# Turning the last third of x by DMA in units 5 and 6 of a fused hash-attention and SwiGLU kernel

## The chip, the cores and the metric

The kernel runs on one core of a Trainium2 chip. The metric is the device time of one execution in microseconds (us), lower is better. The engines are PE (TensorE, matrix multiplication; PEld is its weight load), DVE (VectorE), ACT (ScalarE), POOL (GpSimd) and SP (SyncE, which here only issues DMAs). Each engine works through its own queue in order; semaphores order work between engines.

## The reference, cut to what matters

```python
# q, k, v: 4 batches x 8 heads x 768 positions x 64; proj: 64 x 6
q_bucket, k_bucket = 6 sign bits of q @ proj and of k @ proj
scores = where(q_bucket == k_bucket, q @ k.T / 8, -1e9)
attn_out = softmax(scores) @ v                       # with 1e-9 in the denominator
x = attn_out as 3072 tokens x 512
xn = x / sqrt(mean(x * x) + 1e-6) * rms_g
out = (silu(xn @ w_gate) * (xn @ w_val)) @ w_out     # d_ff = 1536
```

The output is float32, 3072 x 512.

## The kernel before, in words

**Units.** The 3072 tokens are worked in eight units of 384 (half a batch each; `u` = 0 to 7). Attention for a unit runs over 8 heads, two heads making a pair (`hp` = 0 to 3). Each head takes three steps, so a unit has `NS` = 24 steps. In a step PE makes scores (L349), ACT exponentiates them (L361), and PE multiplies probabilities by v (L374) into `o_ps`. What a unit's attention leaves is `x[u]`, 128 partitions x 3 thirds x 512, so that a third (`c` = 0, 1, 2) is 128 tokens.

**From attention to x.** `attn_out` (L382) runs once for each pair: DVE adds a mean of v (L388) and takes a reciprocal (L393), then the engine handed in, POOL by default, multiplies (L395) into `x`. For pairs 0 to 2 POOL also makes the squares (L401), which DVE sums later (L417). For pair 3 DVE makes squares and sums itself (`sumsq_dve`, L411, one instruction for each third). If the engine is DVE, `attn_out` calls `sumsq_dve` at once; otherwise a later step, `s_step`, does. For the last pair of a unit `o_step` stands at step 2 of the next unit's 24 and `s_step` at step 4. Before the change only unit 0 and unit 7 hand DVE to the last pair.

**From x to xnT.** `norm` (step 4) sums the squares over pairs (L439), POOL takes the power -1/2 (L443), and DVE scales each third to float16 `xn`. The feed-forward part needs x transposed, `xnT`, with the gain vector `rms_g` multiplied in. There are two ways. `turn_x` lets PE transpose four 128x128 blocks into a PSUM bank (L467), which DVE evicts with the gain (L473). `turn_dma` lets SP issue one DMA transpose from `xn` to `xnT` (L431); then the gain is multiplied in by `norm` (L452 in place of L460). `ONDMA` says how many thirds of a unit go by DMA. They are issued at step 5, one behind the other on SP's queue.

**Feed-forward beside attention.** While unit u+1 runs its attention, PE works off a list of pieces: the output projection of unit u-1 (`project`, L513, nine pieces of four matmuls), the turns of unit u by PE, and then 24 gate and 24 value halves of unit u (L484). All 384 tokens of `xnT` are read by each gate matmul, so the first gate of a unit needs all three thirds. A planner, `spread`, gives each piece a cost (a projection piece 4 x 216, a turn 220, a gate half 324) and deals the pieces over the steps so that their sum grows evenly. For a third that goes by DMA in units below 6 an empty piece of cost 220 stands where the turn would be.

**Queues and buffers.** SP issues loads, the small sends of hash bits (L308), DMA transposes and stores (L526) in the order in which the program lists them. Projections, turns, gates, values, hashes and means take their PSUM banks in turn from a pool of three (`g`). `xnT` has two buffers, `xn` one.

Of the kernel before, what the change touches and what calls it, by code (L numbers as in the profile page):

```python
# [16 lines left out]
H = 8  # L17
# [16 lines left out]
def kernel(  # L34
# [388 lines left out]

    rstds = {}

    ONDMA = {2: 2, 3: 2, 4: 2, 5: 2, 6: 2, 7: 1}

    def turn_dma(u, c):
        if c == 0:
# [16 lines left out]
    def norm(u):  # L446
# [3 lines left out]
        for c in range(3 if 0 < u < 7 else 2):  # L450
            if c < ONDMA.get(u, 0):
                nc.vector.scalar_tensor_tensor(  # L452
# [141 lines left out]
    order = [(0, 0), (0, 1), (1, 0), (1, 1)]  # L594
# [3 lines left out]
    def at(w, s, f, *a):  # L598
        plan[NS * w + s].append(lambda: f(*a))
# [117 lines left out]
    TX = 37  # L717

    LAGS = (0, 0, 0, 0, 0, 1, 1)
    sqs = {}  # L720

    def o_step(u, hp, *eng):
# [12 lines left out]
    for n, (u, h) in enumerate(order):  # L735
        t = 3 * n + 4 - ((u, h) == (0, H - 1))
        for part in range(2):
            at(0, t + part, av, u, h, part)
        if h % 2:
            if (u, h) == (0, H - 1):  # L740

                at(0, t + 1, o_step, u, h // 2, nc.vector)
                at(0, t + 1, norm_scale, u)
                at(0, t + 1, nc.vector.tensor_scalar_mul, gcol, gcol, float(DMODEL) ** 0.5)
                at(0, t + 2, hash_only, 1, 1)
                at(0, t + 2, hash_signs, 1, 1)
                at(0, t + 2, norm, u)
                at(0, TX-1, norm_third, u, 2, nc.scalar.mul)
                at(0, TX + 1, send_pair, 1, 1)
                for c in range(3):  # L750
                    at(0, TX, turn_x, u, c, c == 2)
                continue
            if (u, h) == order[-1]:
                at(0, t + 1, o_step, u, h // 2, nc.vector)
                continue

            steps = [(t + 1, o_step), (t + (3 if h == 7 else 4 if u == 7 else 6), s_step)]
            for s, step in steps:
                if s < 2 * NS or s % NS in (2, 4) or (step is o_step and (u, h // 2) in AHEAD):
                    at(0, s, step, u, h // 2)  # L760
                else:
                    late.append((s, step, u, h // 2))
# [42 lines left out]
    def spread(t0, n, pieces):  # L805
        fixed = [SCORES + (AV if (t - 1) % 3 < 2 else 0) for t in range(t0, t0 + n)]
        extra = [(t, *inserts.pop(t)) for t in range(t0, t0 + n) if t in inserts]
        total = sum(fixed) + sum(p[0] for p in pieces) + sum(e[1] for e in extra)
        i, done = 0, 0
        for s in range(n):  # L810
            done += fixed[s]
            while i < len(pieces):
                weight, whole, steps = pieces[i]
                full = done + weight // 2 > total * (s + 1) // n
                if extra and whole and t0 + s >= extra[0][0] and (full or extra[0][1] > MEAN):
                    _, weight, *step = extra.pop(0)
                    place(t0 + s, step)
                    done += weight
                    continue
                if full:  # L820
                    break
                done += weight
                for delay, *step in steps:
                    at(0, t0 + s + delay, *step)
                i += 1
        for _, _, *step in extra:
            place(t0 + n - 1, step)
        assert i == len(pieces)

    for u in range(7):  # L830
# [9 lines left out]
        at(0, t0 + 4, norm, u)  # L840
        for c in range(ONDMA.get(u, 0)):
            at(0, t0 + 5, turn_dma, u, c)
        pieces = []
        for i in range(9):
# [5 lines left out]
            if i in (6, 7):  # L850
                thirds = ((0,), (1, 2))[i - 6]
                for c in thirds:
                    if c >= ONDMA.get(u, 0):
                        pieces.append((TURN, False, [(0, turn_x, u, c)]))
                    elif u < 6:
                        pieces.append((TURN, False, []))
        lag, after = LAGS[u - 1 : u + 1]
        spread(t0 + lag, NS + after - lag, pieces + gates)
# [89 lines left out]
```

## Time and profile before

| What | Value |
|---|---|
| median of 3 runs | 326.93 us (326.87 to 327.19) |
| the profiled execution's own time | 326.68 us |
| its span, first to last instruction | 324.9 us |
| mean granted TensorE clock | 0.999 |
| scores on PE (L349) | 384 matmuls |
| transposes of x on PE (L467) | 52 matmuls, 4.7 us busy, mean 219 ns |
| their evictions by DVE (L473) | 11, mean 688 ns |
| DMA transposes (L431) | 11, 1202 to 2021 ns each on SP |
| x by POOL (L395) | 30, mean 837 ns |
| x by DVE (L395) | 2, mean 558 ns |
| xn by DVE with the gain (L452) | 11, mean 748 ns |
| xn by DVE without it (L460) | 11, mean 615 ns |

The span runs from the first to the last instruction; the execution's own time also holds 1.78 us around it. Busy times of an engine are sums over its instructions. Matmuls overlap, so the mean of one is longer than its share of PE's time. In a timeline, rows that follow one another on one engine and line are merged (x4 is four instructions), and an idle time ahead of a row stands in brackets with what ended it.

### The profile page before, as it was taken

What the parts mean: (1) busy time and instruction counts of PE and PEld (TensorE: products, weight loads), DVE (VectorE), ACT (ScalarE), POOL (GpSimd) and SP (SyncE); (2) the same over time, 40 slices, a digit from 0 to 9 for tenths busy, and PEclk for the clock granted to TensorE, in tenths of its full rate; (3) what the DMA queues carried; (4) which work ended last, traced back from release to release, by engine and by line L of the source; (5) the groups of instructions that cost most, each with busy time, mean ns of one, the idle gap of its engine ahead of it and who ended that gap; (6) DMA issues with size and microseconds to landing.
All of it is one profiled execution on the core that took longest, in us unless ns stands there. A gap on an engine that the chain in (4) does not pass through costs nothing.

```text
span 324.9 us, 7772 instructions
## 1 busy us (share of the span) xinstructions
PE 319.9 (98%) x2955; PEld 194.4 (60%) x2955; DVE 229.7 (71%) x512; ACT 228.4 (70%) x333; POOL 157.6 (49%) x204
## 2 busy tenths in 40 slices
PE   8999999999999999999999999999999999999996
PEld 3676666656566565655566565655666556665554
DVE  5887876859888568874888568785677536673870
ACT  7999887667688676776767776777777768744322
POOL 4999759955974363731883621752582111221000
PEclk9999999999999999999999999999999999999999
DMA  7942999988428864055547056002100030003002
GB/s 208 360 168 85 226 216 195 192 159 151 103 38 158 157 136 88 6 94 156 89 100 145 35 125 120 7 5 66 72 4 3 1 99 34 0 2 105 10 2 97
DMA packets 85741, 32.63 MB, mean 100 GB/s; under 512 B 70908, under 2 KB 82632, under 8 KB 85704
## 3 DMA queue, kind: packets, MB, share of 16 engines
q1 hardware_dynamic: 81800, 27.35, 36.1%
q0 software_dynamic: 3680, 4.72, 8.5%
q8 instruction: 23, 0.38, 0.5%
q14 instruction: 14, 0.11, 0.1%
q10 hardware_dynamic: 224, 0.07, 0.1%
HBM read 28.58 MB, written 6.29 MB: 107 GB/s over the span
## 4 chain that ended last, share of the span: by engine, by line
PE 98%; ACT 1%; DVE 0%; issue 0%
PE s_ps L349 20%; PE g_ps L484 19%; PE v_ps L484 19%; PE y_ps L513 18%; PE o_ps L374 11%; PE d_ps L218 2%; PE t_ps L156 2%; PE d_ps L238 2%; PE z_ps L580 1%; PE x_ps L467 1%; PE y_ps L532 1%; PE m_ps L333 1%; ACT psb L361 1%; DVE kT L158 0%; PE s_ps L156 0%
## 5 line engine op out<-in xcount | busy, mean ns | idle before, releaser
L361 ACT ACTIVATE psb<-s_ps,ebias 128x768 f16<-128x768 f32 x192 | 167.7, 900 | 20.0 <-PE s_ps L349 19.2
L349 PE MATMUL s_ps<-QK 128*128 128x384 f16 (+1 forms) x384 | 93.5, 326 | 1.2 <-ACT psb L361 1.1
L492 ACT ACTIVATE t<-g_ps 128x384 f32<-128x384 f32 x96 | 47.2, 492 | 52.2 <-PE g_ps L484 50.5
L484 PE MATMUL g_ps<-xnT,wg 128*128 128x384 f16 x384 | 82.7, 326 | 0.0
L484 PE MATMUL v_ps<-xnT,wv 128*128 128x384 f16 x384 | 81.8, 326 | 0.0
L501 DVE SCALAR_TENSOR_TENSOR a<-t,g_ps 128x384 f32<-128x384 f32 x96 | 53.0, 552 | 28.9 <-ACT t L492 27.2
L395 POOL TENSOR_TENSOR x<-otmp,rcp 128x384 f32<-128x384 f32 x30 | 25.1, 837 | 96.2 <-DVE rcp L393 95.8
L513 PE MATMUL y_ps<-wo,ht 128*128 128x512 f16 x276 | 67.7, 379 | 0.0
L502 DVE SCALAR_TENSOR_TENSOR ht<-a,v_ps 128x384 f16<-128x384 f32 x96 | 53.2, 554 | 11.5 <-PE v_ps L484 3.6
L374 PEld LDWEIGHTS <-psb 128*128 128x128 f16 x1152 | 51.9, 97 | 15.7 <-issue 1.2
L374 PE MATMUL o_ps<-vl,psb 128*128 128x65 f16 x1152 | 55.8, 193 | 0.0
L349 PEld LDWEIGHTS <-QK 128*128 128x128 f16 (+1 forms) x384 | 34.8, 98 | 33.7 <-issue 7.9
L484 PEld LDWEIGHTS <-wg 128*128 128x128 f16 x384 | 35.2, 97 | 21.2
L484 PEld LDWEIGHTS <-wv 128*128 128x128 f16 x384 | 35.1, 97 | 20.8 <-issue 0.2
L513 PEld LDWEIGHTS <-ht 128*128 128x128 f16 x276 | 24.9, 98 | 23.0
L525 ACT COPY ysb<-y_ps 128x512 f32<-128x512 f32 x23 | 13.5, 587 | 15.8 <-PE y_ps L513 15.8
L388 DVE TENSOR_TENSOR otmp<-o_ps,cvb 128x390 f32<-128x390 f32 x32 | 17.8, 557 | 7.1 <-PE o_ps L374 7.1
L208 POOL CAST QK<-qT 64x768 f16<-64x768 f32 x20 | 16.5, 823 | 10.3 <-DVE qT L195 9.5
L401 POOL TENSOR_TENSOR sq<-x 128x384 f32<-128x384 f32 x24 | 19.9, 828 | 1.9
L208 POOL CAST QK<-kT 64x768 f16<-64x768 f32 x20 | 16.4, 822 | 5.2 <-DVE kT L195 3.1
L473 DVE TENSOR_TENSOR xnT<-x_ps,gcol 128x512 f16<-128x512 f16 x11 | 7.4, 688 | 15.1 <-PE x_ps L467 15.0
L195 DVE STREAM_TRANSPOSE kT<-kL 128x192 f32<-128x192 f32 x32 | 16.4, 516 | 0.0
(85 smaller groups left out, 274.9 us busy)
## 6 DMA issues: line engine op xcount, KB each, us to landing
vn<-in_v_dram SPq DMA_DIRECT2D x16, 384.0 KB
out_dram<-ysb SPq DMA_DIRECT2D x23, 256.0 KB
qL<-in_q_dram SPq DMA_DIRECT2D x40, 96.0 KB
kL<-in_k_dram SPq DMA_DIRECT2D x40, 96.0 KB
kn<-in_k_dram SPq DMA_DIRECT2D x5, 384.0 KB
qn<-in_q_dram SPq DMA_DIRECT2D x5, 384.0 KB
wg<-in_moe_w_gate_dram POOLq DMA_DIRECT2D x2, 768.0 KB, 9.4
wv<-in_moe_w_val_dram POOLq DMA_DIRECT2D x2, 768.0 KB, 11.7
```

Source lines behind the costliest of these rows:

```text
L208: nc.gpsimd.tensor_copy(QK[b, 2 * hp + hh, "h"][0:64, o : o + S], src[64 * hh : 64 * hh + 64, :])
L349: nc.tensor.matmul(ps[:, j, 0:HALF], QK[b, h, "h"][rows, S + jt * 128 : S + (jt + 1) * 128], QK[b, h, "h"][rows, half * HALF : (half + 1) ...
L361: nc.scalar.activation(psb[u, h][:, 2 * ch : 2 * ch + 2, :], sps.pop((u, i))[:, :, 0:HALF], AF.Exp, bias=ebias, scale=ESCALE,)
L374: nc.tensor.matmul(o[:, c, hh, 0:65], psb[u, h][:, jt, c * 128 : (c + 1) * 128], vls[b % 2][:, h, 2 * (jt % 3) + jt // 3 if b in PARITY el ...
L388: nc.vector.tensor_add(tmp[:, :, :, 0:65], o[:, :, :, 0:65], cvb[b % 2][:, 2 * hp : 2 * hp + 2, 0:65].unsqueeze(1).to_broadcast([128, 3, 2 ...
L395: eng.tensor_mul(xd.rearrange("p c (h d) -> p c h d", h=2), tmp[:, :, :, 0:64], r.to_broadcast([128, 3, 2, 64]),)
L401: eng.tensor_mul(sq, xd, xd)
L484: nc.tensor.matmul(ps, w[:, kt, fs], xnT[u][:, kt, :], start=(kt == 0), stop=(kt == 3))
L492: nc.scalar.activation(t, fbank[u, ft, "g_ps"], AF.Tanh, scale=0.5)
L501: nc.vector.scalar_tensor_tensor(out=a, in0=t, scalar=1.0, in1=g, op0=ALU.add, op1=ALU.mult)
L502: nc.vector.scalar_tensor_tensor(out=ht[u][:, ft, :], in0=a, scalar=0.5, in1=vv, op0=ALU.mult, op1=ALU.mult)
L513: nc.tensor.matmul(y, ht[u][:, ft, c * 128 : (c + 1) * 128], wo[:, ft, :], start=(ft == 0), stop=(ft == NF - 1),)
```

## The change

Two edits. First, units 5 and 6 turn all three thirds of x by DMA. Their third `c` = 2 leaves `turn_x` and goes to `turn_dma`, as a third DMA transpose behind the other two at step 5; `norm` therefore scales it with the gain. In unit 5 an empty piece keeps the turn's place in the plan; in unit 6 (`u < 6` is false) none does. Second, for the last pair of units 5 and 6 `o_step` is handed DVE: DVE multiplies x and then makes the squares and their sums at once at step 2, and there is no `s_step` at step 4.

```diff
-    ONDMA = {2: 2, 3: 2, 4: 2, 5: 2, 6: 2, 7: 1}
+    ONDMA = {2: 2, 3: 2, 4: 2, 5: 3, 6: 3, 7: 1}
...
     LAGS = (0, 0, 0, 0, 0, 1, 1)
+
+    XDVE = (5, 6)
     sqs = {}
...
-            if (u, h) == order[-1]:
+            if (u, h) == order[-1] or u in XDVE and h == H - 1:
                 at(0, t + 1, o_step, u, h // 2, nc.vector)
                 continue
```

## The prediction

> **What bounds the kernel now.** I read the totals and the chain that ended last first, because they say whether any engine but PE can matter.
>
> ```profile
> PE 319.9 (98%) x2955; PEld 194.4 (60%) x2955; DVE 229.7 (71%) x512; ACT 228.4 (70%) x333; POOL 157.6 (49%) x204
> ...
> PE 98%; ACT 1%; DVE 0%; issue 0%
> ```
>
> PE is busy 319.9 of 324.9 us, and 98% of the chain is PE's own work, one instruction behind the other. So PE time that is taken out shortens the span one for one, and a new wait on PE lengthens it one for one. Work added to DVE, POOL or SP costs nothing until PE waits for it. Then I read the timeline around the two places where a turn by PE goes away. Unit 5 first (columns: start, length, engine, line, operation):
>
> ```profile
> 224.35 2.55 SPq L431 DMA_TRANSPOSE xnT<-xn  x2
> ...
> 226.83 0.47 PEld L374 LDWEIGHTS <-psb 128*128 128x128 f16 x9
> ...
> 227.26 1.03 PE L513 MATMUL y_ps<-wo,ht 128*128 128x512 f16 x4
> ...
> 228.29 0.47 PEld L374 LDWEIGHTS <-psb 128*128 128x128 f16 x9
> ...
> 228.72 0.39 PE L467 MATMUL x_ps<-ident,xn 128*128 128x128 f16 x4
> ...
> 228.95 1.03 PE L513 MATMUL y_ps<-wo,ht 128*128 128x512 f16 x4
> 229.15 0.69 DVE L473 TENSOR_TENSOR xnT<-x_ps,gcol 128x512 f16<-128x512 f16 x1 [3.05 <-PE x_ps L467]
> ...
> 229.97 0.58 PEld L484 LDWEIGHTS <-wg 128*128 128x128 f16 x4
> ```
>
> The reader is to see two things. The turn of the last third (L467) stands alone among PE's work, ahead of the last projection piece. And the first gate weights (L484, 229.97) are the point by which all of xnT must have landed. Unit 6, same columns:
>
> ```profile
> 257.21 0.19 DVE L393 RECIPROCAL rcp<-otmp 128x6 f32<-128x6 f32 x1
> ...
> 261.06 3.33 SPq L431 DMA_TRANSPOSE xnT<-xn  x2
> ...
> 265.06 0.47 PEld L374 LDWEIGHTS <-psb 128*128 128x128 f16 x9
> ...
> 265.72 1.03 PE L513 MATMUL y_ps<-wo,ht 128*128 128x512 f16 x4
> ...
> 266.75 0.59 PEld L484 LDWEIGHTS <-wg 128*128 128x128 f16 x4
> ```
>
> **PE's turns removed: the gain.** Two turns go, (5,2) and (6,2), four 128x128 transposes each. Their price is not the mean of 219 ns that the group's row gives, since matmuls overlap. I take it from starts. Without a turn, the step from the first attention load (L374) to the first projection matmul is 227.26 - 226.83 = 0.43 us; with one it is 228.95 - 228.29 = 0.66, and in unit 6 265.72 - 265.06 = 0.66. So a turn costs 0.23 us of PE, two cost 0.46. Bounds: 0.22 (start of L467 to start of L513 in unit 6) and 0.39 (the modelled busy time of the four). I take 0.23, since starts are recorded and ends modelled. The Trainium skill prices this otherwise: the page "TensorE: Matmul & The Clock Gate", section "Part 4: PE-mode transpose", gives about 275 ns for a transpose in a kernel's context; eight would be 2.2 us. The row of starts disagrees here, four in 0.23 us.
>
> PE's removed work takes two DVE evictions with it (L473, 0.69 us each) and one bank each from the rotation of three; the gate's banks are then older ones, so no bank wait appears. PE has no idle time in these stretches that this could give back.
>
> **The third turn by DMA: the risk.** In each unit SP issues one more DMA_TRANSPOSE. Two last 2.55 us, so a third starts some 2.57 us after the first and ends 1.24 later; the longest of the eleven in the trace took 2.02, the shortest 1.20. How long after its issue it has landed, no wait shows, so I bound it. From below by the DMA bytes of unit 5's second turn, whose issue ended at 226.90 (columns: stretch, then busy time by engine, granted clock, DMA share, GB/s):
>
> ```profile
> 226.75:227.00 0.25, 0.25 (x4) 0.12 (x3) 0.00 (x0) 0.20 (x1) 0.00 (x0) 1.00 0.24 52
> 227.00:227.25 0.25, 0.25 (x10) 0.25 (x9) 0.00 (x0) 0.06 (x1) 0.00 (x0) 1.00 1.10 217
> 227.25:227.50 0.25, 0.25 (x8) 0.13 (x5) 0.00 (x0) 0.25 (x1) 0.00 (x0) 1.00 1.04 210
> ```
>
> The bytes move for about 0.7 us after the issue, so 0.7 is the low end. From above by unit 4, where the issue ended soonest before the gate and PE waited for nothing:
>
> ```profile
> 187.45 2.58 SPq L431 DMA_TRANSPOSE xnT<-xn  x2
> ...
> 191.36 0.45 PEld L484 LDWEIGHTS <-wg 128*128 128x128 f16 x4
> ```
>
> 191.36 - 190.03 = 1.33 is the high end. I take the middle, 1.0.
>
> Unit 5: first issue 224.35, third 226.92 to 228.16, landed 228.9 to 229.5, say 229.2. The gate's load moves up to 229.97 - 0.23 = 229.74. Margin 0.25 at the worst, 0.5 as taken. No wait.
>
> Unit 6 depends on when x is normalized. The same code on DVE alone is seen in unit 7:
>
> ```profile
> 291.27 0.19 DVE L393 RECIPROCAL rcp<-otmp 128x6 f32<-128x6 f32 x1
> 291.50 0.56 DVE L395 TENSOR_TENSOR x<-otmp,rcp 128x384 f32<-128x384 f32 x1
> ...
> 292.85 0.17 DVE L439 TENSOR_REDUCE ss<-ssp 128x3 f32<-128x15 f32 x1
> ```
>
> Reciprocal to sum takes 1.58 us there. Unit 6 of before needs 1.89 (257.21 to 259.10), with the multiplication on POOL (0.83). So x comes 0.31 earlier: first issue 260.75, third 263.32 to 264.56, landed 265.3 to 265.9. The load moves up to 266.52. Margin 0.6 at the worst. In unit 5 the gain on x is nothing: before, a turn of K (L195 at 220.57) ran on DVE while POOL multiplied; now it stands behind the squares. 1.58 plus its pitch of 0.37 (217.45 to 217.82, two in a row) is 1.95, and before it was 222.43 - 220.47 = 1.96.
>
> **What stands behind the third issue on SP.** In unit 5 four sends of hash bits (from 227.00) and two stores (230.01) go about 1.26 us later. The bits are for head 5 of batch 3. Gates start at 230.13 in unit 5 and 266.91 in unit 6, 24 steps on, so a step is 1.53 us; the scores that read the bits are issued five steps on, at 237.8, and the bits land by 228.2 + 2.92 + 1.33 = 232.5. A store's buffer comes round again about 30 us later. No load stands near behind. Cost nothing; cover 5 us. In unit 6 two stores go at most 0.1 later.
>
> **DVE and POOL.** Added on DVE in each unit: x by 0.56 (row of unit 7) and the third part of xn with the gain vector, 0.70 in place of 0.48; removed 0.69. Net +0.09 of some 37 us a unit, at 71% busy. The third part is ready at 225.7 and 262.1, over 1 us before SP comes to it. POOL loses 0.83 a unit; nothing waits for it but x itself. Nothing for all of this; if the cover went, the most is the 0.7 us by which the third part would be late, and SP would still have to be idle first.
>
> **The plan of unit 6.** The place of its turn is not kept by an empty piece, as in unit 5 (u < 6). The planner's total falls by 220, and worked through its sums three halves of gates and values move one step (179 to 178, 182 to 181, 185 to 184). Nothing is added. From below nothing, since PE is busy through these steps; from above 0.8, the longest wait of scores for an exponential in the trace. I take nothing: these steps hold the same kinds of pieces as their neighbours.
>
> **Sum.** The profiled execution took 326.68 (span 324.9 and 1.78 around it). 326.68 - 0.46 = 326.22. The median of the runs is 0.25 above that execution, so 326.93 - 0.46 = 326.47.
>
> **Rivals.** What a measurement of this kernel can tell from no change is about 0.2%, 0.65 us: faster is below 326.28, slower above 327.58.
>
> *More than the starts show.* If the four transposes hold PE for their modelled 0.39, the gain is 0.78: 326.15. Against it, the next matmul starts inside those 0.39. Should each cost its whole row of 219 ns, eight give 1.75: 325.18; the starts speak plainly against it. By the Trainium skill's 275 ns (page and section above) it would be 324.73.
>
> *One slow issue in each unit.* Two of the eleven turns took 1.82 and 2.02, in units 2 and 6, so the third may come 0.82 late. Unit 5 lands at 228.98 + 1.0 = 229.98, 0.24 past the load; unit 6 at 266.38, still in time. -0.46 + 0.24: 326.71. For it, it has happened in unit 6.
>
> *Late completion.* The farthest row for a landing is the last store: issue ended 322.79, program at 324.9, 2.11 us. With this the waits are 228.16 + 2.11 - 229.74 = 0.53 and 264.56 + 2.11 - 266.52 = 0.15: 327.15. Unit 4's 1.33 speaks against it. The Trainium skill, page "DMA: Bandwidth & Descriptors", section "Anatomy of one DMA", has a fixed cost of about 2.0 us, most of it the receipt after the last byte, stated for GpSimd's path; unit 4 does not bear it out.
>
> *Nothing gained.* PE's freed 0.46 turns into waits for exponentials: 326.93. ACT waits 0.6 us for PE at each of these steps, which speaks against it.
>
> *Slower: SP backs up on three in a row.* If a third transfer finds the queue full and two of the three issues take 2.02, it ends 1.64 later: unit 5 lands at 230.80, unit 6 at 267.20. PE stands at the gate's first load for 1.06 and 0.68, and all its queue with it. 1.74 - 0.46 = +1.28: 328.21. It decides once landing is over 0.5 later than reckoned in unit 5. For it, slow issues occur with only two in a row; against, three of five pairs ran at 1.2 each.
>
> **How the numbers follow.** Forecast 326.47, 0.46; more gain 0.19 (326.15 with 0.16, 325.18 with 0.03); one slow issue 0.12; late completion 0.05; nothing gained 0.03; SP backs up 0.15. Faster is 0.19, slower 0.15, the rest 0.66. The range 326.0 to 327.6 leaves out 325.18 and 328.21, together 0.18; the forecast alone, with its 0.22 to 0.39 a turn and no wait, is 326.15 to 326.5.
>
> **What would show it.** L467 with 44 transposes, L473 with 9, thirteen DMA_TRANSPOSE; in unit 5 the step from L374 to L513 at 0.43; SP's three in 3.8 us; PE's waits holding no DMA; x on DVE four times. I am wrong if PE or its weight load is idle ahead of L484 at about 229.7 or 266.3, or if an issue is longer than 1.3.

## The result, and the profile after

The changed kernel takes 327.65 us (median of 14 runs, 327.17 to 328.45) against 327.19 for the kernel before, measured beside it (14 runs, 326.87 to 327.42). The medians differ by 0.46. The ratio of the runs is 1.0018 (0.6 us), interval 1.001 to 1.0026: slower by 0.3 to 0.9 us, where 0.46 faster was forecast. The profiled execution took 327.85 with a span of 326.1. One run of the later repeat of this kernel ("changed, again" below) took 670.75 us and is in none of the ratios.

The page of the changed kernel, totals and chain:

```profile
PE 319.9 (98%) x2947; PEld 193.8 (59%) x2947; DVE 230.1 (71%) x512; ACT 228.2 (70%) x333; POOL 155.7 (48%) x202
...
PE 95%; DMA 2%; ACT 1%; SPq 1%; issue 0%
```

PE lost its eight transposes (2955 to 2947) and is still busy 319.9 us. The total doesn't show the gain, since the modelled ends of matmuls cover part of PE's new waits: the first gate of unit 6 comes 0.73 later, and its row in the timeline of unit 6 below has 0.56 of that as idle time. What is new is in the chain: DMA and SP now stand in it. By line, 1% is the transfer of xnT, 1% SP's turns (L431), and 1% a load of q at the start, which the change doesn't touch. Unit 5 in the timeline, the rows that answer to those of before:

```profile
224.58 3.87 SPq L431 DMA_TRANSPOSE xnT<-xn  x3
...
228.53 0.47 PEld L374 LDWEIGHTS <-psb 128*128 128x128 f16 x9
...
228.97 1.03 PE L513 MATMUL y_ps<-wo,ht 128*128 128x512 f16 x4
...
230.00 0.58 PEld L484 LDWEIGHTS <-wg 128*128 128x128 f16 x4
```

Three turns in 3.87 us, the step from L374 to L513 at 0.44, and the gate's load comes without a wait: unit 5 is as forecast. Unit 6:

```profile
260.77 5.29 SPq L431 DMA_TRANSPOSE xnT<-xn  x3
...
265.08 0.47 PEld L374 LDWEIGHTS <-psb 128*128 128x128 f16 x9
...
265.52 1.03 PE L513 MATMUL y_ps<-wo,ht 128*128 128x512 f16 x4
...
267.40 0.45 PEld L484 LDWEIGHTS <-wg 128*128 128x128 f16 x4 [0.92 <-issue]
267.43 0.81 PE L484 MATMUL g_ps<-xnT,wg 128*128 128x384 f16 x4 [0.56 <-DMA xnT<-xn]
```

Here three turns took 5.29, and PE stood idle until xnT had landed. The instructions of L431 in this stretch (durations: shortest, median, longest in ns, then the first and the last start) say which kind of lateness it is:

```profile
L431 SPq DMA_TRANSPOSE xnT<-xn x3: 1207/1216/2681, 260.8 to 264.8; - x3
```

One of the three took 2.68. The last one starts 4.0 behind the first, which two turns of 1.2 don't fill, so the long one is not the last: it is the first (260.77 to 263.45). It was not a third that found the queue full.

Setting the starts of the 384 score matmuls of the two profiles side by side gives the whole account:

| Place | PE later (+) or earlier (-), us |
|---|---|
| start of the program, first loads | +0.24 |
| unit 5's turn gone | -0.22 |
| unit 6's turn gone | -0.22 |
| unit 6, first gate waits for xnT | +0.73 |
| unit 6, scores four us later | +0.28 |
| last matmul to the end of the span (3.01 before, 3.38 after) | +0.37 |
| sum; the spans differ by 1.2 | +1.18 |

The first row is no work of the change, as far as the profiles show: the first scores come 0.1 to 1.0 later than in the profile of before in all the other profiles of this study, also in the three that turn no third more by DMA. The forecast had the two rows with a minus. The other three are what the experiments had to explain.

**The gap of 0.28.** ACT of the changed kernel behind unit 6's first gate, then PE in the same stretch:

```profile
268.67 0.89 ACT L361 ACTIVATE psb<-s_ps,ebias 128x768 f16<-128x768 f32 x1
270.18 0.49 ACT L492 ACTIVATE t<-g_ps 128x384 f32<-128x384 f32 x1 [0.62 <-PE g_ps L484]
270.56 1.69 ACT L361 ACTIVATE psb<-s_ps,ebias 128x768 f16<-128x768 f32 x2
```

```profile
270.58 0.81 PE L484 MATMUL v_ps<-xnT,wv 128*128 128x384 f16 x4
271.51 0.48 PE L349 MATMUL s_ps<-QK 128*128 128x384 f16 x2
```

The four value matmuls follow one another every 0.16, so the scores could have started at 271.23; they start at 271.51. They take over a PSUM buffer which the first exponential of the 270.56 row frees at 271.46. That exponential had its scores at 268.9, but the tanh (L492) stood ahead of it in ACT's queue and waited for its gate until 270.18. It is the tanh of the gate half that the planner moved from step 179 to 178. In the kernel before, the same tanh (270.26) stands behind both exponentials:

```profile
267.76 0.49 ACT L492 ACTIVATE t<-g_ps 128x384 f32<-128x384 f32 x1 [0.39 <-PE g_ps L484]
268.15 1.69 ACT L361 ACTIVATE psb<-s_ps,ebias 128x768 f16<-128x768 f32 x2
270.26 0.49 ACT L492 ACTIVATE t<-g_ps 128x384 f32<-128x384 f32 x1 [0.42 <-PE g_ps L484]
```

**The end.** SP's waits on the last line of the program (total, times, longest), the kernel before and the changed one:

```profile
SPq L943 <- DMA out_dram<-ypart: 1.4, 3, 0.6
```

```profile
SPq L945 <- DMA out_dram<-ypart: 1.8, 2, 1.2
```

At the end SP checks eight semaphores one behind the other, 0.06 us each. In the kernel before it waits three times, for the last three stores in turn, and the last is the eighth check. In the changed kernel the last store is the second check, and six more follow it, already fulfilled, which take 0.37 together.

### The profile page after: what moved, and what is told of

It is laid out like the page before. It is cut to its first block, busy times and chain, and to the rows that moved or that the text cites. A ratio compares the mean times of both kernels' runs of the same rounds, so it can differ in the third digit from the quotient of the medians.

```text
span 326.1 us, 7761 instructions
## 1 busy us (share of the span) xinstructions
PE 319.9 (98%) x2947; PEld 193.8 (59%) x2947; DVE 230.1 (71%) x512; ACT 228.2 (70%) x333; POOL 155.7 (48%) x202
## 4 chain that ended last, share of the span: by engine, by line
PE 95%; DMA 2%; ACT 1%; SPq 1%; issue 0%
PE s_ps L349 20%; PE g_ps L484 19%; PE v_ps L484 19%; PE y_ps L513 17%; PE o_ps L374 10%; PE d_ps L218 2%; PE t_ps L156 2%; PE d_ps L238 2%; DMA qn<-in_q_dram 1%; ACT psb L361 1%; PE y_ps L532 1%; PE x_ps L467 1%; DMA xnT<-xn 1%; SPq L431 1%; PE m_ps L333 1%; PE z_ps L580 0%
## 5 line engine op out<-in xcount | busy, mean ns | idle before, releaser
L492 ACT ACTIVATE t<-g_ps 128x384 f32<-128x384 f32 x96 | 47.1, 491 | 53.4 <-PE g_ps L484 51.9
L513 PE MATMUL y_ps<-wo,ht 128*128 128x512 f16 x276 | 67.7, 379 | 0.0
L395 POOL TENSOR_TENSOR x<-otmp,rcp 128x384 f32<-128x384 f32 x28 | 23.4, 837 | 89.8 <-DVE rcp L393 89.4
L374 PEld LDWEIGHTS <-psb 128*128 128x128 f16 x1152 | 51.9, 97 | 15.7 <-issue 1.2
L374 PE MATMUL o_ps<-vl,psb 128*128 128x65 f16 x1152 | 55.8, 193 | 0.0
L513 PEld LDWEIGHTS <-ht 128*128 128x128 f16 x276 | 24.8, 98 | 23.0
L443 POOL TENSOR_TENSOR rstd<-ss,mhalf 128x3 f32<-128x3 f32 x8 | 6.9, 865 | 23.1 <-DVE ss L439 22.5
```

Source lines behind the costliest of these rows:

```text
L374: nc.tensor.matmul(o[:, c, hh, 0:65], psb[u, h][:, jt, c * 128 : (c + 1) * 128], vls[b % 2][:, h, 2 * (jt % 3) + jt // 3 if b in PARITY el ...
L395: eng.tensor_mul(xd.rearrange("p c (h d) -> p c h d", h=2), tmp[:, :, :, 0:64], r.to_broadcast([128, 3, 2, 64]),)
L492: nc.scalar.activation(t, fbank[u, ft, "g_ps"], AF.Tanh, scale=0.5)
L513: nc.tensor.matmul(y, ht[u][:, ft, c * 128 : (c + 1) * 128], wo[:, ft, :], start=(ft == 0), stop=(ft == NF - 1),)
```

## The experiments

Each is an edit of the changed kernel, save the two named "before", which edit the kernel before. "Gate" is the delay that unit 6's first gate adds to PE's starts, "gap" the delay of the scores behind it, "tail" the time from the start of the last matmul to the end, all from one profile. Ratios are to the kernel before on the same chip.

| Kernel | Ratio (interval) | Gate | Gap | Tail |
|---|---|---|---|---|
| unit 5 only | 1.0008 (0.9999 to 1.0016) | 0 | 0 | 3.47 |
| unit 6 only, place kept | 1.0015 (1.0007 to 1.0024) | 0.20 | 0 | 3.48 |
| place kept | 1.0003 (0.9995 to 1.0012) | 0.45 | 0 | 3.38 |
| transfers moved | 1.0013 (1.0000 to 1.0025) | 0 | 0.28 | 3.40 |
| tail restored | 0.9999 (0.9991 to 1.0008) | 0.18 | 0.28 | 3.02 |
| mended | 1.0003 (0.9988 to 1.0018) | 0 | 0 | 3.04 |
| before, one DMA more | 1.0009 (1.0000 to 1.0018) | 0 | 0 | 3.46 |
| x on DVE only | 0.9998 (0.9989 to 1.0006) | 0 | 0 | 3.01 |
| before, 42 rows more | 1.0004 (0.9993 to 1.0015) | 0 | 0 | 3.01 |
| mended, 30 rows | 0.9995 (0.9983 to 1.0006) | 0 | 0 | 3.01 |
| unit 5 only, tail restored | 1.0002 (0.9993 to 1.0011) | 0 | 0 | 3.02 |
| place kept, tail restored | 0.9994 (0.9983 to 1.0006) | 0.42 | 0 | 3.02 |
| mended, again | 0.9993 (0.9980 to 1.0006) | 0 | 0 | 3.03 |
| changed, again | 1.0015 (1.0006 to 1.0024) | 0.65 | 0.28 | 3.38 |

The intervals are wide beside the effects, 0.2 to 0.7 us of 327. So the verdicts rest on the profiles, one for each kernel, and the times have to be in keeping with them.

### Unit 5 only

```diff
-    ONDMA = {2: 2, 3: 2, 4: 2, 5: 3, 6: 3, 7: 1}
+    ONDMA = {2: 2, 3: 2, 4: 2, 5: 3, 6: 2, 7: 1}
-    XDVE = (5, 6)
+    XDVE = (5,)
```

> Unit 5 alone: three thirds by DMA and x by DVE there, unit 6 as before. In the changed kernel's profile unit 5 gained 0.22 us on PE and its three turns took 1.25, 1.21 and 1.22 on SP. If all the loss is unit 6's, this is 0.2 us faster than before (ratio near 0.9993), with no wait of PE for a DMA at a gate. If three turns in a row fill SP's queue in themselves (the rival), unit 5 loses too in some runs: ratio 1.000 or above.

The turns of unit 5 took 1.25, 1.21 and 1.22, PE's starts came 0.22 earlier there, and no gate waited. Yet the time went up. Neither side of the expectation had the reason: the tail is 3.47 in place of 3.01. With the end of the program counted, the sum is -0.22 + 0.46 = +0.24; measured 1.0008, +0.26.

### Unit 6 only, its place in the plan kept

```diff
-                    elif u < 6:
+                    elif u < 6 or c == 2:
...
-    ONDMA = {2: 2, 3: 2, 4: 2, 5: 3, 6: 3, 7: 1}
+    ONDMA = {2: 2, 3: 2, 4: 2, 5: 2, 6: 3, 7: 1}
-    XDVE = (5, 6)
+    XDVE = (6,)
```

> Unit 6 alone has three thirds by DMA and x by DVE, and an empty piece of cost 220 keeps its turn's place in the plan; unit 5 as before. Theory: the late third turn costs 0.73 at the gate, the turn by PE that goes gives 0.22, and the 0.28 that PE waited for an exponential four us later is gone because no piece moves: about 0.5 us slower than before (ratio 1.0015), one long turn of over 2 us in unit 6 and PE waiting some 0.6 for xnT there, no gap ahead of the scores after it. Rival (the 0.28 follows from the late gate, not from the moved pieces): the gap stays, 0.8 slower (1.0024).

The gap is gone though the gate still waits, so it follows from the moved pieces. The long turn was 2.17 this time and the gate lost only 0.20. The ratio came as expected, but not by the expected sum: -0.22 + 0.20 + 0.47 (tail) = +0.45 for a measured +0.5.

### Place kept, and transfers moved

The first keeps the place alone (the `elif` above, both units). The second leaves the plan and cuts filler matmuls, which run where PE has nothing to do, into narrower ones of the same total width:

```diff
-    def idle(n, new=None):
+    def idle(n, new=None, cut=1):
...
-        for _ in range(n):
-            nc.tensor.matmul(ps, ones_sq, ones_row, start=True, stop=True)
+        w = 512 // cut
+        for _ in range(n * cut):
+            nc.tensor.matmul(ps[:, 0:w], ones_sq, ones_row[:, 0:w], start=True, stop=True)
-    idle(6)
+    idle(6, None, 2)
...
-        idle(n, lambda name: hole[0])
+        idle(n, lambda name: hole[0], 4)
```

> The whole change, with an empty piece of cost 220 that keeps the place of unit 6's turn. Theory: 0.28 us less than the changed kernel, so about 0.2 us slower than before (ratio 1.0006); the gate wait of unit 6 stays at 0.7. Rival (the gap follows from the late gate): as the changed kernel, 1.0018.

> The whole change, with the filler matmuls of the first steps cut into narrower ones of the same total width: 42 more rows in PE's instruction stream, no other work. In both profiles 22 transfers of 16 KB on the instruction queue come at even counts of PE's rows, and each of the four slow turns has one of them within it. With 42 rows more each transfer comes some 2.4 us earlier in PE's work, in unit 6 at about 259 in place of 261.5, before the first turn is issued. Theory (the transfer makes the turn slow): three turns of 1.2 in unit 6, no wait for xnT, 0.7 us less than the changed kernel, about 0.2 faster than before (ratio 0.9995). Rival (three turns in a row fill the queue): a turn of over 2 us stays in unit 6 and the ratio stays at 1.0018.

PE of "place kept" in unit 6:

```profile
267.05 0.81 PE L484 MATMUL g_ps<-xnT,wg 128*128 128x384 f16 x4 [0.29 <-DMA xnT<-xn]
...
270.19 0.81 PE L484 MATMUL v_ps<-xnT,wv 128*128 128x384 f16 x4
270.84 0.49 PE L349 MATMUL s_ps<-QK 128*128 128x384 f16 x2
```

The wait for xnT is still there, and the scores follow the values at once (270.19 + 4 x 0.16). The ratio, 1.0003, is below the 1.0006 expected, and below the sum by the profile: -0.44 + 0.45 + 0.37 is +0.38, measured +0.1 (interval -0.2 to 0.4). The rows of L431 in unit 6 in "place kept", then in "transfers moved":

```profile
L431 SPq DMA_TRANSPOSE xnT<-xn x3: 1207/1217/2420, 260.7 to 264.5; - x3
```

```profile
L431 SPq DMA_TRANSPOSE xnT<-xn x3: 1200/1217/1272, 260.7 to 263.3; - x3
```

In the second the instruction transfer starts at 259.88, ahead of the first turn's issue at 260.67; all three turns take 1.2 to 1.27, at the same time of issue, and the gate doesn't wait. (The traces hold 23 such transfers each, not 22.) PE of "transfers moved":

```profile
266.28 0.49 PE L349 MATMUL s_ps<-QK 128*128 128x384 f16 x2
266.61 0.81 PE L484 MATMUL g_ps<-xnT,wg 128*128 128x384 f16 x4
...
269.76 0.81 PE L484 MATMUL v_ps<-xnT,wv 128*128 128x384 f16 x4
270.69 0.48 PE L349 MATMUL s_ps<-QK 128*128 128x384 f16 x2
```

The gate follows the scores at once, and the gap of 0.28 stands behind the values (269.76 + 4 x 0.16 is 270.41). The two costs are told apart: each edit took away its own and left the other. The ratio of "transfers moved", 1.0013, is not the 0.9995 expected. That took the gate's 0.73 of one profile off the measured time, while other profiles show as little as 0.2. By its own profile the sum is -0.44 + 0.28 + 0.39 = +0.23 (measured +0.4, interval 0 to 0.8).

### Tail restored, and the kernel before with one DMA more

```diff
-        nc.sync.dma_start(out=rows_of(u, c), in_=ysb)
+        n = 2 if u in (3, 4, 5) and c else 1
+        for i in range(n):
+            cols = slice(i * DMODEL // n, (i + 1) * DMODEL // n)
+            nc.sync.dma_start(out=rows_of(u, c)[:, cols], in_=ysb[:, cols])
```

The other has the same lines in the kernel before, with `n = 2 if (u, c) == (5, 2) else 1`.

> The whole change, with six stores of units 3 to 5 split into two halves each: six DMAs more, no bytes more. At the end of the program SP goes through eight semaphores in a fixed order, 0.06 us each, and each new DMA moves the last one to land by one place in that order. Before, the last was eighth; with the change's two DMAs more it is second and six checks follow it (the profile: 0.37 us more from the last matmul to the end). With eight more it is eighth again. Theory: 0.37 less than the changed kernel, about 0.1 us slower than before (ratio 1.0003), and 3.0 us from the last matmul to the end. Rival (the tail is chance from run to run): as the changed kernel, ratio 1.0018.

> The kernel before, with one store of unit 5 split into two halves and nothing else. Theory of the end: the last DMA becomes first in the order of the eight semaphores, seven checks of 0.06 follow it, 0.45 us slower than before (ratio 1.0014), all of it after the last matmul. Rival (the number of DMAs does not matter): ratio 1.000.

SP's waits at the end, tail restored and then the kernel before with one DMA more:

```profile
SPq L948 <- DMA out_dram<-ypart: 1.4, 3, 0.6
```

```profile
SPq L946 <- DMA out_dram<-ypart: 1.9, 1, 1.9
```

The first has the order of the kernel before, the second waits once, at the first check, with seven behind it. Over the sixteen profiles of the study the tail is 3.01 to 3.04 where the number of DMAs is that of before or eight more (nine profiles), 3.46 to 3.48 with one more (three) and 3.38 to 3.40 with two more (four). So this cost goes with a count and is not chance. The times agree: 0.9999 for the first (sum -0.44 + 0.18 + 0.28 = 0.0), +0.3 (interval 0 to 0.6) for the second, where 0.45 was expected.

### X on DVE only

```diff
-    ONDMA = {2: 2, 3: 2, 4: 2, 5: 3, 6: 3, 7: 1}
+    ONDMA = {2: 2, 3: 2, 4: 2, 5: 2, 6: 2, 7: 1}
```

> The second edit alone: x of the last pair of units 5 and 6 by DVE with its squares at once, two thirds by DMA as before. Every theory: PE does the same work and waits for nothing new, the number of DMAs is that of before, ratio 1.000 within 0.0007. In unit 6 the first DMA transpose is issued some 0.3 us earlier than before.

0.9998 (0.9989 to 1.0006), and behind the first 85 us PE's starts keep one distance to those of before, 0.94 to 0.98. In unit 6 the first turn is issued at 261.69, so 0.3 earlier beside PE's work, as expected. The second edit by itself costs and gains nothing that shows.

### The three mended

Place kept, transfers moved and tail restored together; run twice, the second time beside the changed kernel on one chip.

> The whole change with all three costs taken away: the empty piece in the plan of unit 6, the 42 more rows for PE that move the instruction transfers, and the six split stores that restore the order at the end. Theory: only the two turns taken from PE are left, 0.44 us faster than before (ratio 0.9987). Rival (something else in the change costs time that the profiles do not show): not faster than before, 1.000 or above.

> The kernel with the three costs taken away, again, now beside the changed kernel on one chip. Theory: 0.9 less than the changed kernel and 0.4 us faster than before (ratio 0.9987), with a profile as its first one: every turn of 1.5 or less, no wait of PE at a gate, 3.0 us from the last matmul to the end. If something not yet found costs time, three or four runs of twelve over 328.2 come again and the ratio is 1.000.

> The changed kernel again, on the same chip. Theory: 0.4 to 0.9 us slower than before (ratio 1.0012 to 1.0027), one turn over 2.0 us in unit 6 with a 16 KB instruction transfer within it, PE waiting 0.2 to 0.7 at its gate, the gap of 0.28 behind it, 3.37 us from the last matmul to the end.

PE loses nothing and gains 0.22 in each unit in both profiles of the mended kernel. On the one chip its median is 326.90, that of the changed kernel 327.86, that of the kernel before 327.24: 0.96 less than the changed kernel, where 0.9 was expected; by the two ratios it is 0.7. By their sizes in the profiles (0.28, 0.37 and 0.2 to 0.7) the three costs are 0.85 to 1.35. So they account for the difference as far as these runs can tell. That the mended kernel beats the kernel before, by the 0.4 expected or at all, is not shown. Both medians lie 0.33 to 0.34 below, but the ratios are 1.0003 and 0.9993 and both intervals hold 1: 4 of its 24 runs took over 328.2, and of the 58 runs of before beside them none did.

### Where the long runs come from

In the kernel before, the fillers alone are cut; and the mended kernel without the cut of `idle(6)`:

> The kernel before with the 42 more rows of PE alone (filler matmuls cut, no work added). In the kernel with the three costs taken away, four of twelve runs took 327.8 to 329.0, more than any but one of the runs of before. If the cut fillers bring these, this kernel has some runs above 328.2 too, with a median near before (ratio 1.000). If not (the rival: the two turns by DMA bring them), all its runs lie between 326.7 and 328.2.

> The three costs taken away as in the mended kernel, but only the fillers of steps 34 to 36 cut, not those ahead of the first transpose: 30 rows more. Theory: the instruction transfer of unit 6 starts at some 259.9 and is nearly over when the first turn is issued, so no turn takes over 1.5 us, PE's wait at unit 6's gate is 0, and the kernel is 0.4 us faster than before (ratio 0.9987). If the cut fillers ahead of the first transpose brought the slow runs of the mended kernel, there are none here; if they come again, they come from the fillers of steps 34 to 36 or from the turns.

The first had one run above 328.2 of twelve, with two of 35 in the kernel before beside it; the second had none. That settles nothing about the long runs, and their cause stays open. The second was expected at 0.9987 with no wait, and came at 0.9995 with one. With 30 rows, a transfer of unit 3 moved to 150.82, into that unit's first turn (rows of L431, then PE):

```profile
L431 SPq DMA_TRANSPOSE xnT<-xn x2: 1207/1741/2275, 150.0 to 152.4; - x2
```

```profile
154.97 0.81 PE L484 MATMUL g_ps<-xnT,wg 128*128 128x384 f16 x4 [0.19 <-DMA xnT<-xn]
```

A unit that the change doesn't touch, with two turns, now has a turn of 2.28 us and a wait at its gate, which puts PE's starts 0.35 later. So neither three turns in a row nor x on DVE is needed for a slow turn.

### Unit 5 only and the whole change, with the tail restored

The first is "unit 5 only" with seven stores split, the second "place kept" with six.

> Unit 5 alone, with seven stores split so that the last DMA is eighth again in SP's order at the end. Theory: the one turn taken from PE is all that is left, 0.22 us faster than before (ratio 0.9993), 3.0 us from the last matmul to the end, and 0.45 less than unit 5 alone without the splits. Rival: as unit 5 alone was, ratio 1.0008.

> The whole change with the empty piece in unit 6's plan and the order at the end restored, the instruction transfer left where it is. Theory: -0.44 for the two turns, +0.2 to +0.7 for the wait at unit 6's gate, which was 0.2, 0.45 and 0.7 in the profiles so far: ratio between 0.9993 and 1.0008, one turn of 2.0 us or more in unit 6, no gap ahead of the scores behind it, 3.0 us from the last matmul to the end.

Profiles as expected (-0.22 and no wait; gate 0.42, no gap, tail 3.02 in both). The times tell neither from the kernel before: 1.0002 and 0.9994. The gain of one turn, 0.22, is below what twelve runs can show.

## Why the prediction was wrong, point by point

**PE's turns removed: right.** 0.23 each was forecast from starts; it is 0.22 in every profile with the edit. The rivals with 0.39 a turn or 0.22 a transpose fall, and with them the Trainium skill's 275 ns ("TensorE: Matmul & The Clock Gate", "Part 4: PE-mode transpose").

**Unit 5: right.** First issue, three in 3.9 us, third part ready, sends and stores behind it: none made PE wait, in any of the eleven profiles that have this edit. By the landing measured below it was close: 228.45 + 1.35 is 229.80, and the gate's load started at 230.00. That x gains nothing in unit 5 and 0.3 in unit 6 was right too (260.77 in place of 261.06).

**Landing: the step took 1.0 us after the issue's end, between 0.7 and 1.33.** It is the high end: in the six profiles where unit 6's gate waited, its load starts 1.33 to 1.37 after the third issue ended. That took 0.3 of the margin. With it even the slow issue that the prediction priced among its rivals, 0.82, is no longer in time in unit 6: 264.56 + 0.82 + 1.35 is 0.21 past 266.52, and the two profiles whose long turn ahead of a waiting gate was 2.11 and 2.17 lost 0.18 and 0.20 there.

**"first issue 260.75, third 263.32 to 264.56": this is the step that failed.** The first issue came as forecast (260.77), but the third ended at 266.06, because the first took 2.68 where 1.24 was taken. A slow issue was priced among the rivals at the 0.82 of the trace's longest, without asking what made two of eleven turns slow. That was to be seen in the profile of before. Its page has the queue, and in the DMA packets of the trace it is 23 transfers of 16 KB:

```profile
q8 instruction: 23, 0.38, 0.5%
```

They come every 8 to 20 us, and one of them started 0.36 and 0.41 us after the issue of just the two slow turns. They go by a count of PE's instructions: in this profile 5,508 weight loads and matmuls start between the first transfer and the last, 250 for each step on average (179 to 300), and the transfer of unit 6 stands behind 4,952 to 4,965 of them in all sixteen profiles. All 197 turns of these profiles, by when a transfer started:

```
transfer starts after the turn's issue by      turns   duration of the turn, us
0.26 to 0.80 us                                 17     1.75 to 2.68
earlier and still running, 0 to 0.2, 1.0 to 1.1 16     1.23 to 1.69
none from issue to 1.2 us after                164     1.19 to 1.34
```

In unit 6, one turn took 1.69 to 2.68 in all eleven profiles with the fillers as they were, and none over 1.39 in the five with cut fillers.

In the changed kernel the transfer began at 261.52, 0.76 after the issue, and lasted 1.50. Stretches of the changed kernel (then busy time by engine, granted clock, DMA share, GB/s; a packet's whole time is booked where it starts, so a share can be above 1):

```profile
261.50:261.75 0.25, 0.25 (x4) 0.12 (x3) 0.25 (x1) 0.00 (x0) 0.00 (x0) 1.00 0.38 66
...
262.25:262.50 0.25, 0.25 (x3) 0.11 (x2) 0.00 (x0) 0.25 (x1) 0.00 (x0) 1.00 1.02 202
262.50:262.75 0.25, 0.25 (x3) 0.10 (x1) 0.00 (x0) 0.25 (x1) 0.00 (x0) 1.00 1.64 117
262.75:263.00 0.25, 0.25 (x3) 0.10 (x1) 0.00 (x0) 0.25 (x2) 0.00 (x0) 1.00 0.00 0
263.00:263.25 0.25, 0.25 (x3) 0.11 (x2) 0.00 (x0) 0.25 (x1) 0.00 (x0) 1.00 0.12 8
263.25:263.50 0.25, 0.25 (x3) 0.13 (x2) 0.00 (x0) 0.13 (x1) 0.00 (x0) 1.00 0.07 9
263.50:263.75 0.25, 0.25 (x3) 0.15 (x2) 0.00 (x0) 0.00 (x0) 0.00 (x0) 1.00 0.08 10
```

The first row is the instruction transfer (66 GB/s for a quarter of a us is 16 KB). Then the turn's bytes start as usual, and at 262.50 the DMA engines are booked at 1.64 for 117 GB/s: four of the turn's 512 packets took 1.05 to 1.18 us, where the median is 0.018. All four end at 263.79 or 263.80, some 0.8 after the transfer. The other bytes of these rows come at 8 to 10 GB/s, while the turns of unit 5 (shown in the prediction) are done in three such rows. So it was not SP's queue that was full, as the rival "SP backs up on three in a row" had it, and not the third; in "transfers moved" three in a row took 1.2 to 1.27 each. The Trainium skill, page "Runtime: NRT & Kernel Launch", section "Terms", says that each engine's instruction memory is refilled in blocks of 16 KiB; the size agrees. And the Trainium skill's page "DMA: Bandwidth & Descriptors", section "Queues, rings and completion order", has a DMA engine switch between queues at packet boundaries only. Long packets beside the transfer are in keeping with that, but which engine carried it, and what holds the four until 0.8 after its end, no trace here shows. That a transfer in this place makes the turn slow is shown; how it does so stays open.

The second edit brought the two closer to the worst distance: with x 0.3 earlier, the first turn was issued 0.76 instead of 0.41 ahead of the transfer, and took 2.68 in place of 2.02. Whether the kernel would be faster without that edit is open, since no run has three turns without it. In the profile of before the same collision cost nothing, since the second and last turn's issue ended 2.36 us ahead of the gate's load.

**"The plan of unit 6 ... I take nothing": 0.28.** The step argued that nothing is added and that PE is busy throughout. It didn't look at the queue behind the moved piece. The gate's tanh is issued on ACT ahead of the next exponential, and one step earlier it holds that exponential back by waiting for its gate.

**The end of the program was not in the sum: 0.37.** The prediction counted what the two more DMAs take on SP's queue, under "What stands behind the third issue on SP", and nothing else of them. They also move the last DMA in the order of the checks at the end.

**The sum.** -0.44 + 0.28 + 0.37 and 0.2 to 0.7 for the gate, which differs from profile to profile, is +0.4 to +0.9; measured +0.6 by the ratio (0.33 to 0.85), and +0.5 (0.2 to 0.8) the second time. DVE, POOL and stores cost nothing, as forecast.

## What to carry to other kernels

When a rare slow instruction would break a margin, look for what else happened in just those cases before pricing it by chance: here it was tied to an instruction count, and so came back in every profile until the count was moved. A piece taken from a plan moves its neighbours, and each neighbour's followers on the other engines have to be read too. Where gains are tenths of a microsecond, compare the time from the last matmul to the end as well: it depends on the number of DMAs.

## What the runs showed of the hardware that was not expected

An instruction transfer of 16 KB lengthens a DMA transpose from 1.2 to as much as 2.7 us if it starts 0.26 to 0.80 us after the issue (17 turns of 17, 1.75 to 2.68). Cutting the fillers of the kernel before into 42 more rows of PE moved the transfer of unit 6 from 261.47 to 259.49, though PE itself ran 0.59 later in that profile. The place of the last store among the eight checks at the end is worth up to 0.47 us (3.01 to 3.48). And the profiles differ by up to 1.0 us at the first scores; the 1.0 is that of "place kept, tail restored", whose edits all come later.
